# Decode attention beside a gated feed-forward on one core: the order of the first weights, narrower streams, and where a few transfers stand in the queue

## The chip, the core and the metric
The kernel runs on one of the eight cores of a Trainium2 chip. A core has a matrix engine (TensorE, in the profile PE, its weight loads PEld), a vector engine (VectorE, DVE), an engine for pointwise functions (ScalarE, ACT), a general engine (GpSimd, POOL) and one that mainly issues transfers (SyncE, SP). They run side by side and meet through semaphores. Sixteen DMA engines move data between the chip's memory and the core's SBUF; matmul results go to eight PSUM banks. The metric is device time in microseconds for one execution.

## The reference
Four decode requests (B = 4, one token each, D = 512). The token is normalised, and two branches start from it:

```python
xn = _layernorm(x, axis=-1)
# attention over the last W = 4096 positions, 32 query heads on 8 key/value heads
q = (xn @ wq)                                   # 512 -> 32*128
scores = einsum("bhqd,bhkd->bhqk", q, k) * (128 ** -0.5)
o = einsum("bhqk,bhkd->bhqd", softmax(scores), v)
A = o.reshape(4, 1, 4096) @ wo                  # 4096 -> 512
# gated feed-forward, F = 1792
Bf = (silu(xn @ w_gate) * (xn @ w_up)) @ w_down
out = x + A + Bf
```

All inputs and the output are bf16. What has to be read: 33.5 MB of keys, 33.5 MB of values, 4.2 MB each of `wq` and `wo`, 1.8 MB each of the three feed-forward matrices: 81 MB for very little arithmetic.

## The kernel before
The 32 pairs of request and key/value head are taken two at a time, in ND = 16 passes (two requests, one head). A pass d has a K tile and a V tile of 2 MB each: 64 blocks of 128 positions by 128 numbers. Both have two buffers in SBUF, bank d % 2.

**The preamble.** ScalarE and VectorE normalise x, TensorE transposes it into `XnT` (128 x 4 chunks, line 279). TensorE then forms gate (56 matmuls), up (56) and Q (128), each with a 128x128 block of weights as the stationary operand and `XnT` as the moving one. `XnT` is padded with zeros from the 4 columns that matter to WIDE = 64 columns, so each of these matmuls streams 64. Each writes 60 columns beyond its own into PSUM, zeros there, which accumulate without harm. VectorE then turns gate and up into the product `guT` (lines 280 to 288) and Q into the layout `QZ` (290 to 294); line 295 sets free the PSUM banks that gate and up have used, so that transposes may write there.

**The loop.** Eight rounds of two passes. On TensorE a pass is: wait for K of this pass; 32 transposes of the first half of K; the maxima of the pass before; PV of the second half of pass d - 2; the mask and 32 score matmuls; the shift of the pass before; 32 transposes of the second half; denominators and PV of the first half of pass d - 1; 32 score matmuls. VectorE copies each eight transposes out of PSUM (line 300), takes row maxima, and normalises. ScalarE does one exponential per pass. For the passes before the first one, P and V hold constants that GpSimd has written, and a signal from GpSimd (line 208) counts as their V having landed.

**SP's queue.** All big transfers are issued by SP, in the written order, and each wait holds up all that stands behind it (lines 225 to 248): W_gate, W_up, W_Q in two DMAs, K0, K1, the first half of V0, all without a wait; then a wait for the first PV of the loop (`s_pv` 1, since the second half's buffer is used up to then), the second half of V0; then in turn K of pass d, once the transposes of pass d - 2 are done (line 214, `s_tr`), and V of pass d - 1, once the PV of the pass two before it in its buffer is done (line 218, `s_pv`). Behind the loop come W_down, the last V in two halves, and W_O in four pieces of 16, 10, 4 and 2 rows of 128 KB (WO_CUTS, line 243).

**The tail.** TensorE adds x and the down-projection, finishes the last pass, transposes the attention output, and multiplies by W_O row by row as its pieces land (64 matmuls). VectorE rounds the sum, and two small transfers write the output.

## Time and profile before

| | |
|---|---|
| median of 3 runs | 200.82 us (200.08 to 201.39) |
| the profiled execution | 200.82 us, its span 198.3 us |
| granted TensorE clock, mean | 0.991 |
| HBM read | 81.01 MB, 409 GB/s over the span |
| TensorE busy | 170.0 us (86%) |
| VectorE busy | 112.1 us (57%) |
| ScalarE / GpSimd busy | 16.6 / 10.4 us |

The profile page is of one execution. It gives busy time by engine, the span in 40 slices (digits are tenths of a slice; below them the gigabytes per second moved), the chain of work that ended last, followed back from the end, the costliest groups of instructions with their count, busy time, mean duration and idle time ahead, and the issues of transfers with the time from issue to landing. Line numbers (L346 and so on) are those of the kernel; L346 is the helper `mm` through which nearly all matmuls go, so groups of that line are told apart by their tiles: `wq_sb`, `wg_sb`, `wu_sb` are the weights of Q, gate and up, `kbuf` and `vbuf` K and V, `kT` the transposed K, `ps_s` scores, `ps_o` PV. In a listing by time the columns are start, length, engine, line, operation, tiles, count, and in brackets the idle time ahead with its releaser. "SPq" is SP's queue: the time an issue takes there. A transfer lands when the last of its 16 parts has.

### The profile page before, as it was taken

How to read it: one execution, taken by the hardware profiler on the slowest of the kernel's cores; microseconds unless marked ns; L12 is line 12 of the kernel's file. 1: busy time of each engine (PE TensorE's matmuls, PEld its weight loads, DVE VectorE, ACT ScalarE, POOL GpSimd, SP SyncE). 2: the span in 40 equal slices, each digit the busy share in tenths (PEclk: the TensorE clock that was granted, in tenths of full speed). 3: DMA queues.
4: the chain of work that ended last, by engine and by line, in shares of the span. 5: the costliest groups of instructions: out<-in, count | busy, mean ns of one | idle time of the engine just before them, and what ended most of it. 6: DMA issues, size and time to landing. Idle time of an engine off the chain costs nothing.

```text
span 198.3 us, 8098 instructions
## 1 busy us (share of the span) xinstructions
PE 170.0 (86%) x3634; PEld 150.7 (76%) x3634; DVE 112.1 (57%) x246; ACT 16.6 (8%) x26; POOL 10.4 (5%) x23
## 2 busy tenths in 40 slices
PE   0383789999999989898989898989898989898865
PEld 0383778989889888887888788878887888786633
DVE  1010027777776867666667676767676767675110
ACT  6600001010101010100001010101010101010000
POOL 8920000000000000000000000000000000000000
PEclk9999999999999999999999999999999999999988
DMA  6999998999999999999999999999999999999991
GB/s 206 425 444 420 433 436 329 345 393 421 423 426 440 433 426 430 423 436 426 450 426 430 423 436 423 453 423 426 430 426 433 430 446 426 430 428 417 438 404 50
DMA packets 6223, 81.12 MB, mean 409 GB/s; under 512 B 700, under 2 KB 712, under 8 KB 968
## 3 DMA queue, kind: packets, MB, share of 16 engines
q1 hardware_dynamic: 6200, 81.01, 96.7%
q8 instruction: 6, 0.10, 0.2%
q10 hardware_dynamic: 16, 0.01, 0.0%
q14 instruction: 1, 0.01, 0.0%
HBM read 81.01 MB, written 0.00 MB: 409 GB/s over the span
## 4 chain that ended last, share of the span: by engine, by line
DMA 59%; PE 34%; issue 2%; SPq 2%; DVE 2%; DVEq 0%
DMA kbuf<-in_A_k_cache_dram 51%; PE ps_kt L384 17%; PE ps_s L346 9%; DMA wo_sb<-in_A_wo_dram 8%; PE ps_o L346 6%; PE ps_acc L346 2%; DVE kT L300 1%; SPq L229 1%; SPq L223 1%; SPq L245 0%; DVE y_sb L341 0%; SPq L225 0%; SPq L226 0%; DVEq L299 0%
## 5 line engine op out<-in xcount | busy, mean ns | idle before, releaser
L300 DVE COPY kT<-ps_kt 128x1024 bf16<-128x1024 bf16 x128 | 79.5, 684 | 21.4 <-PE ps_kt L384 21.3
L384 PE MATMUL ps_kt<-ident,kbuf 128*128 128x128 bf16 x1024 | 62.8, 220 | 8.0 <-DMA kbuf<-in_A_k_cache_dram 8.0
L384 PEld LDWEIGHTS ps_kt<-ident,kbuf 128*128 128x128 bf16 x1024 | 57.3, 98 | 13.1 <-issue 12.9
L346 PE MATMUL ps_o<-p,vbuf 128*128 128x64 bf16 x1120 | 38.6, 194 | 0.1
L346 PEld LDWEIGHTS ps_s<-qz,kT 128*128 128x128 bf16 x1024 | 31.4, 98 | 6.7 <-issue 3.6
L346 PEld LDWEIGHTS ps_o<-p,vbuf 128*128 128x128 bf16 x1120 | 35.3, 98 | 1.4 <-issue 0.2
L346 PE MATMUL ps_s<-qz,kT 128*128 x1024 | 34.7, 192 | 1.2
L265 ACT ACTIVATE p<-ps_s 128x512 bf16<-128x512 f32 x17 | 10.1, 597 | 161.2 <-PE ps_s L346 161.2
L305 DVE TENSOR_REDUCE rm<-ps_s 128x8 bf16<-128x512 f32 x17 | 11.8, 692 | 19.3 <-PE ps_s L346 19.3
L346 PE MATMUL ps_acc<-xnT,wq_sb 128*128 128x64 bf16 x128 | 7.2, 242 | 4.1 <-DMA wq_sb<-in_A_wq_dram 4.1
L346 PEld LDWEIGHTS ps_acc<-xnT,wq_sb 128*128 128x128 bf16 x128 | 6.9, 132 | 4.4 <-DMA wq_sb<-in_A_wq_dram 4.4
L346 PE MATMUL ps_o<-p,ones 128*128 128x128 bf16 (+1 forms) x69 | 6.9, 220 | 0.5 <-DVE qz L291 0.5
L316 DVE TENSOR_REDUCE den<-ps_o 128x8 f32<-128x128 f32 x18 | 4.9, 274 | 4.0 <-PE ps_o L346 4.0
L360 PE MATMUL ps_acc<-i,xn 4*128 4x4 f32 x4 | 0.6, 254 | 7.0 <-ACT xn L260 7.0
L291 DVE CAST qz<-ps_acc 128x64 bf16<-128x64 f32 x2 | 0.4, 220 | 11.0 <-PE ps_acc L346 11.0
L346 PE MATMUL ps_s<-dg,ones 8*128 8x512 bf16 x17 | 6.5, 385 | 0.0
L346 PE MATMUL ps_s<-mkc,mkr 2*128 2x512 bf16 x17 | 6.5, 385 | 0.0
L346 PE MATMUL ps_acc<-wo_sb,oP 128*4 128x256 bf16 x64 | 5.4, 339 | 1.3 <-DMA wo_sb<-in_A_wo_dram 1.3
L360 PEld LDWEIGHTS ps_acc<-i,xn 4*128 4x128 f32 x4 | 0.6, 208 | 7.0 <-issue 7.0
L346 PEld LDWEIGHTS ps_acc<-wo_sb,oP 128*4 128x4 bf16 x64 | 3.3, 102 | 3.3 <-DVE oP L339 1.4
L320 DVE TENSOR_TENSOR oT<-ps_o,den 128x8 f32 (+1 forms) x18 | 3.0, 167 | 4.2 <-issue 4.0
L346 PEld LDWEIGHTS ps_o<-p,ones 128*128 128x128 bf16 x69 | 4.6, 98 | 0.9 <-issue 0.9
(62 smaller groups left out, 60.1 us busy)
## 6 DMA issues: line engine op xcount, KB each, us to landing
kbuf<-in_A_k_cache_dram SPq DMA_DIRECT2D x16, 2048.0 KB, 12.6
vbuf<-in_A_v_cache_dram SPq DMA_DIRECT2D x14, 2048.0 KB, 11.2
wq_sb<-in_A_wq_dram SPq DMA_DIRECT2D x2, 2048.0 KB, 19.6
vbuf<-in_A_v_cache_dram SPq DMA_DIRECT2D x4, 1024.0 KB, 9.2
wo_sb<-in_A_wo_dram SPq DMA_DIRECT2D x1, 2048.0 KB, 14.3
wg_sb<-in_B_w_gate_dram SPq DMA_DIRECT2D x1, 1792.0 KB, 7.6
wu_sb<-in_B_w_up_dram SPq DMA_DIRECT2D x1, 1792.0 KB, 11.4
wd_sb<-in_B_w_down_dram SPq DMA_DIRECT2D x1, 1792.0 KB, 15.0
```

The lines of the kernel that those rows point to most:

```text
L223: eng.dma_start(VB[:, a:a + HKN], kv_ap(A_v_cache, d)[:, :, h * HKN:(h + 1) * HKN]).then_inc(done, 16)
L229: eng.dma_start(WQ[:, a:a + NC // 2 * HQ * Dh], wq_ap[:, a:a + NC // 2 * HQ * Dh]).then_inc(d_wq[h], 16)
L265: eng.activation(P[:, d % 2 * PS:d % 2 * PS + SN], ps_S[d % 2][:], ACT.Exp, scale=SCALE).then_inc(s_p, 1)
L291: last = eng.tensor_copy(QZ[:].rearrange("p (k b) c -> p k b c", b=2)[:, :, bp, 0:C].rearrange("p k (j h) -> p k j h", j=2), q_ps.rearrang ...
L300: eng.tensor_copy(KT[:, u * HKN + 1024 * g:u * HKN + 1024 * (g + 1)], kt_ps[g].rearrange("p a b -> p (a b)")).then_inc(s_ev, 1)
L305: eng.tensor_reduce(RM[:], ps_S[bank][:].rearrange("p (t c) -> p c t", c=C), AX.X, ALU.max).then_inc(s_rm, 1)
L316: eng.tensor_reduce(den[:], den_ps.rearrange("p (t c) -> p c t", c=C), AX.X, ALU.add)
L320: eng.tensor_tensor(OT[:, 2 * b:2 * b + 2, ds(r * REP, REP)], O_ps.rearrange("p (j h) -> p j h", j=2), den[:].rearrange("p (j h) -> p j h" ...
L346: return eng.matmul(o, l, r, start=start, stop=stop, skip_group_check=True)
L360: last = eng.transpose(xT_ps[:, c * B:(c + 1) * B], xn[:].rearrange("b (p c) -> b c p", c=NC)[:, c, :], I4[:])
L384: last = eng.transpose(kt_ps[g][:, k, :], KB[:, a:a + 128], ident[:])
```

## The change
Five things are changed together.

- W_Q is issued first and in one DMA, then W_gate and W_up. TensorE forms Q first, then gate and up, and VectorE lays out Q before it works on gate and up.
- `XnT` has 4 columns instead of 64, and the matmuls of Q, gate and up stream these 4. GpSimd no longer zeroes it.
- V of the second pass comes in two halves. The first half is issued when the scores of the first pass are done (`s_sc` 2), the other when V was issued before (`s_pv` 2). Each half has a semaphore, and GpSimd waits for both and then raises the semaphore for which TensorE waits.
- W_O is cut into five pieces (4, 12, 10, 4, 2 rows). The first, 4 rows, is issued behind the first half of V0, ahead of the wait for the loop's first PV.
- The remaining pieces follow at the end as before.

```diff
-    XnT = sb("xnT", [128, NC, WIDE], BF16)
+    XnT = sb("xnT", [128, NC, B], BF16)
...
-    WO_CUTS = (0, 16, 26, 30, 32)
+    WO_CUTS = (0, 4, 16, 26, 30, 32)
...
+    d_vy = [sem("d_vy%d" % h) for h in range(2)]
...
-            eng.memset(XnT[:].bitcast(FP32), 0.0)
...
             eng.engine_nop().then_inc(d_v[1], 32)
+            eng.wait_ge(d_vy[0], 16)
+            eng.wait_ge(d_vy[1], 16)
+            eng.engine_nop().then_inc(d_v[1], 16)
...
+            def load_wo(n):
+                a, b = WO_CUTS[n], WO_CUTS[n + 1]
+                eng.dma_start(WO[:, a:b, :], wo_ap[:, a:b, :]).then_inc(d_wo[n], 16)
+
+            eng.dma_start(WQ[:], wq_ap).then_inc(d_wq, 16)
             eng.dma_start(WG[:], wg_ap).then_inc(d_wg, 16)
             eng.dma_start(WU[:], wu_ap).then_inc(d_wu, 16)
-            for h in range(2):
-                a = h * NC // 2 * HQ * Dh
-                eng.dma_start(WQ[:, a:a + NC // 2 * HQ * Dh], wq_ap[:, a:a + NC // 2 * HQ * Dh]).then_inc(d_wq[h], 16)
             load_k(0)
             load_k(1)
 
             load_v_half(0, 0, d_v[0])
+            load_wo(0)
             eng.wait_ge(s_pv, 1)
             load_v_half(0, 1, d_v[0])
-            for d in range(2, ND):
+            load_k(2)
+            eng.wait_ge(s_sc, 2)
+            load_v_half(1, 0, d_vy[0])
+            eng.wait_ge(s_pv, 2)
+            load_v_half(1, 1, d_vy[1])
+            for d in range(3, ND):
                 load_k(d)
                 load_v(d - 1)
...
-            for n in range(len(d_wo)):
-                a, b = WO_CUTS[n], WO_CUTS[n + 1]
-                eng.dma_start(WO[:, a:b, :], wo_ap[:, a:b, :]).then_inc(d_wo[n], 16)
+            for n in range(1, len(d_wo)):
+                load_wo(n)
...
-            eng.tensor_copy(XnT[:, :, 0:B], xT_ps.rearrange("p (c b) -> p c b", b=B)).then_inc(s_xnT, 1)
-            eng.wait_ge(s_ex, 1)
-            (gate and up to guT: 7 lines)
+            eng.tensor_copy(XnT[:], xT_ps.rearrange("p (c b) -> p c b", b=B)).then_inc(s_xnT, 1)
             eng.wait_ge(s_q, 1)
             for bp in range(2):
                 last = eng.tensor_copy(
...
             last.then_inc(s_qz, 1)
+            eng.wait_ge(s_ex, 1)
+            (gate and up to guT: the same 7 lines)
             eng.engine_nop().then_inc(s_ev, NG)
...
-                        last = mm(o[:, t * B:t * B + WIDE],
+                        last = mm(o[:, t * B:(t + 1) * B],
                                   w[:].rearrange("p c (m t) -> p c t m", t=NF)[:, c, t, :], XnT[:, c, :],
...
+            eng.wait_ge(d_wq, 16)
+            for c in range(NC):
+                for h in range(HQ):
+                    a = (c * HQ + h) * Dh
+                    last = mm(q_ps[:, h * B:(h + 1) * B], WQ[:, a:a + Dh], XnT[:, c, :],
+                              start=(c == 0 and h == 0))
+            last.then_inc(s_q, 1)
             up_gate(WG, ps_kt[0], s_gate, d_wg)
             up_gate(WU, ps_kt[1], s_up, d_wu)
-            for c in range(NC):
-                if c % (NC // 2) == 0:
-                    eng.wait_ge(d_wq[c // (NC // 2)], 16)
-                for h in range(HQ):
-                    a = (c * HQ + h) * Dh
-                    last = mm(ps_acc[:, h * B:h * B + WIDE], WQ[:, a:a + Dh], XnT[:, c, :],
-                              start=(c == 0 and h == 0))
-            last.then_inc(s_q, 1)
```

More of the change, by code (lines that the diff above doesn't have):

```diff
@@ L113, in bass_parallel_sum__sliding_block_cached__swiglu_ffn__decode_kernel @@
     d_x = sem("d_x")
-    d_wq = [sem("d_wq%d" % h) for h in range(2)]
+    d_wq = sem("d_wq")
     d_wg = sem("d_wg")
@@ L278, in _ @@
             eng.wait_ge(s_const, 1)
-            eng.tensor_copy(XnT[:, :, 0:B], xT_ps.rearrange("p (c b) -> p c b", b=B)).then_inc(s_xnT, 1)
+            eng.tensor_copy(XnT[:], xT_ps.rearrange("p (c b) -> p c b", b=B)).then_inc(s_xnT, 1)
+            eng.wait_ge(s_q, 1)
+            for bp in range(2):
+                last = eng.tensor_copy(
+                    QZ[:].rearrange("p (k b) c -> p k b c", b=2)[:, :, bp, 0:C].rearrange("p k (j h) -> p k j h", j=2),
+                    q_ps.rearrange("p (k h b j) -> p k b j h", k=HKV, h=REP, b=2)[:, :, bp])
+            last.then_inc(s_qz, 1)
             eng.wait_ge(s_ex, 1)
@@ L288, in _ @@
             eng.tensor_tensor(guT[:], up_ps.rearrange("p (t b) -> p t b", b=B), gs[:], ALU.mult).then_inc(s_guT, 1)
-            eng.wait_ge(s_q, 1)
-            for bp in range(2):
-                last = eng.tensor_copy(
-                    QZ[:].rearrange("p (k b) c -> p k b c", b=2)[:, :, bp, 0:C].rearrange("p k (j h) -> p k j h", j=2),
-                    q_ps.rearrange("p (k h b j) -> p k b j h", k=HKV, h=REP, b=2)[:, :, bp])
-            last.then_inc(s_qz, 1)
             eng.engine_nop().then_inc(s_ev, NG)
```

## The prediction
> **What bounds the kernel now.** First the page's rows by slice, the traffic, and the chain that ended last.

> ```profile
> DMA  6999998999999999999999999999999999999991
> GB/s 206 425 444 420 433 436 329 345 393 421 423 426 440 433 426 430 423 436 426 450 426 430 423 436 423 453 423 426 430 426 433 430 446 426 430 428 417 438 404 50
> HBM read 81.01 MB, written 0.00 MB: 409 GB/s over the span
> DMA 59%; PE 34%; issue 2%; SPq 2%; DVE 2%; DVEq 0%
> ```

> The transfers are busy nearly from end to end, and 59% of the chain is theirs. Two slices of 4.96 us stand out, 329 and 345 GB/s (29.7 to 39.7 us); the rest holds about 430. Engine times by stretch, whose last three columns are the granted TensorE clock, the DMA share and GB/s, say it more sharply:

> ```profile
> 4.00:30.00 26.00, 16.67 (x266) 15.67 (x267) 3.11 (x11) 4.15 (x7) 7.21 (x6) 1.00 1.01 430
> 30.00:46.00 16.00, 15.82 (x357) 14.04 (x354) 12.00 (x27) 1.19 (x2) 0.00 (x0) 1.00 0.93 359
> 46.00:62.00 16.00, 15.92 (x358) 14.26 (x355) 11.44 (x26) 1.19 (x2) 0.00 (x0) 1.00 1.01 430
> 62.00:172.00 110.00, 101.24 (x2271) 90.77 (x2269) 75.11 (x158) 6.57 (x11) 0.00 (x0) 1.00 1.01 431
> ```

> From 62 to 172 us the traffic runs at 431 GB/s and TensorE is busy 101.2 of 110 us: transfers set the pace. From 30 to 46 us it is the other way round: TensorE has 15.82 of 16 us filled and traffic falls to 359. The shortfall is (431 - 359) x 16 us = 1.15 MB, or 2.7 us of transfer time. Why it idles is in SP's issues (start, length) and in the answers on the landing of single transfers (last column: us from issue to landing; x1 rows of a narrow window):

> ```profile
> 4.39 28.21 SPq L223 DMA_DIRECT2D vbuf<-in_A_v_cache_dram  x2
> 35.63 0.54 SPq L215 DMA_DIRECT2D kbuf<-in_A_k_cache_dram  x1
> 41.02 0.53 SPq L219 DMA_DIRECT2D vbuf<-in_A_v_cache_dram  x1
> ...
> kbuf<-in_A_k_cache_dram SPq DMA_DIRECT2D x1, 2048.0 KB, 25.7
> vbuf<-in_A_v_cache_dram SPq DMA_DIRECT2D x1, 1024.0 KB, 31.6
> vbuf<-in_A_v_cache_dram SPq DMA_DIRECT2D x1, 1024.0 KB, 7.2
> kbuf<-in_A_k_cache_dram SPq DMA_DIRECT2D x1, 2048.0 KB, 9.3
> ```

> The first half of V0 is issued at 4.39 and lands 31.6 us later, at 36.0; by then everything issued early is in. Its second half was issued at about 32.0 (7.2 us, landed 39.2), K2 only at 35.63 (landed 44.9), V1 at 41.02. From there nothing is lost any more: behind K2 come 81.01 MB less 16.25 MB (both gate and up matrices 3.67, W_Q 4.19, K0 to K2 6.29, V0 2.10) = 64.76 MB, and 64.76 / 0.431 = 150.3 us, so the last byte should land at 195.2. It does:

> ```profile
> 176.08 2.02 SPq L245 DMA_DIRECT2D wo_sb<-in_A_wo_dram  x4
> ...
> wo_sb<-in_A_wo_dram SPq DMA_DIRECT2D x1, 1280.0 KB, 16.7
> wo_sb<-in_A_wo_dram SPq DMA_DIRECT2D x1, 512.0 KB, 17.5
> wo_sb<-in_A_wo_dram SPq DMA_DIRECT2D x1, 256.0 KB, 17.7
> ...
> 193.49 2.52 PE ps_acc L346 x30
> ```

> The four issues take 0.5 us each, the last starts near 177.6 and lands 17.7 later, at 195.3. So **the end = landing of K2 + bytes behind it / 431 GB/s**, and the whole change comes down to those two terms. The last chain row shows the tail: rows 16 to 25 of W_O land at 193.45, 2.52 us of matmuls follow, then the output.

> The profiled execution took 200.82 us, of which 198.3 are the span and 2.5 lie around it; 200.82 is also the median of the three runs (200.08 to 201.39), so I subtract from it directly.

> **The change part by part.** *Four rows of W_O* (4 x 128 KB = 0.524 MB) move from behind K2 to ahead of the gated half of V0. At 431 GB/s that is 1.22 us less behind K2: 149.1 instead of 150.3. In front of K2 they land at 36.0 + 1.22 = 37.2, the gated half of V0 (1.049 MB, 2.43 us) no earlier than 39.7, K2 (2.097 MB, 4.87 us) no earlier than 44.5, if its issue stays at 35.63. If an issue into a drained queue sets it, the bounds are these: the first load of the kernel took 7.6 us for 1.835 MB,

> ```profile
> wg_sb<-in_B_w_gate_dram SPq DMA_DIRECT2D x1, 1792.0 KB, 7.6
> ```

> which is 7.6 - 4.26 = 3.3 us beside its bytes, and K2 itself 9.3 - 4.87 = 4.4. By 3.3 K2 can land at 43.8, by 4.4 at 44.9 as now. K2 thus stays between 44.5 and 44.9, and this part alone gives 1.2 to 1.6 us. Each extra issue costs SP 0.5 us at 5 us, where SP then waits till 32 anyway: nothing. Without that wait it would cost 0.5.

> The trace also bears on whether small pieces pay. The 512 KB piece of W_O, issued 0.5 us behind the 1280 KB piece, landed 0.5 + 17.5 - 16.7 = 1.3 us behind it; its bytes take 1.22. [...]

> *Second V in halves.* V1's first half is let go when the scores of the first pass are done, instead of with the second pass's PV. It waits for less than before, so nothing behind it on SP (its other half, then K3, whose own condition comes at 44.6) is held up. It puts 1.05 MB into the queue about 3 us earlier:

> ```profile
> 36.84 1.06 PE L346 MATMUL ps_s<-qz,kT 128*128 x32
> 53.40 0.39 PE L346 MATMUL ps_o<-p,ones 128*128 128x128 bf16 x4
> ```

> 37.9 instead of 41.0. V1 landed at 49.6 and is wanted by the third pass at 53.4, so it was never late, and its new detour over GpSimd's queue (two waits, one signal, nothing queued behind them) has 3.8 us of cover; bare it would cost a few tenths. It keeps the queue filled after K2, where the sum above finds no loss to win back: 0. With K2 late it is what keeps one loss from becoming two.

> *W_Q first, Q before gate and up.* The bytes ahead of K0 are the same 7.86 MB. What TensorE does last before the loop is now "up", not the second half of Q:

> ```profile
> 8.55 3.56 PE L346 MATMUL ps_kt<-xnT,wg_sb 128*128 128x64 bf16 x56 [0.90 <-DMA wg_sb<-in_B_w_gate_dram]
> 12.69 3.60 PE L346 MATMUL ps_kt<-xnT,wu_sb 128*128 128x64 bf16 x56 [0.58 <-DMA wu_sb<-in_B_w_up_dram]
> 19.27 3.59 PE L346 MATMUL ps_acc<-xnT,wq_sb 128*128 128x64 bf16 x64 [2.98 <-DMA wq_sb<-in_A_wq_dram]
> 23.95 3.60 PE L346 MATMUL ps_acc<-xnT,wq_sb 128*128 128x64 bf16 x64 [1.09 <-DMA wq_sb<-in_A_wq_dram]
> 28.88 1.96 PE L384 MATMUL ps_kt<-ident,kbuf 128*128 128x128 bf16 x32 [0.21 <-DMA kbuf<-in_A_k_cache_dram]
> 30.92 1.11 PE L346 MATMUL ps_o<-p,vbuf 128*128 128x64 bf16 x32
> ```

> The last weights landed at 23.95 and will again; "up" with 64 columns took 3.60, the same as half of Q. So the loop stays ready by 27.6 at worst, and its first transposes wait for K0 (3.09 + 25.7 = 28.8) either way. VectorE's gate arithmetic now sits ahead of the signal that frees the transposes' banks: one product of 0.2 us, done by 27.9. W_Q in one DMA saves an issue of 0.4 us that nobody waits for; one GpSimd memset less (0.2 us) likewise. All 0, hidden behind K0; without that cover they would be tenths.

> *Streaming 4 columns.* The matmuls before the loop can only get shorter (up to 3.6 us per group), and K0 hides that. But the rows above hold a trap. A matmul of one shape, 128x64, comes every 3.60 / 64 = 56 ns in Q and every 1.11 / 32 = 35 ns in the loop's PV, and one takes 242 against 194 ns:

> ```profile
> L346 PE MATMUL ps_acc<-xnT,wq_sb 128*128 128x64 bf16 x128 | 7.2, 242 | 4.1 <-DMA wq_sb<-in_A_wq_dram 4.1
> L346 PE MATMUL ps_o<-p,vbuf 128*128 128x64 bf16 x1120 | 38.6, 194 | 0.1
> ...
> 191.00:192.00 1.00, 1.00 (x18) 0.72 (x14) 0.00 (x0) 0.00 (x0) 0.00 (x0) 0.66 0.96 403
> 192.00:193.00 1.00, 1.00 (x12) 0.63 (x10) 0.00 (x0) 0.00 (x0) 0.00 (x0) 0.50 0.95 387
> 193.00:194.00 1.00, 0.94 (x11) 0.34 (x8) 0.00 (x0) 0.00 (x0) 0.00 (x0) 0.50 0.71 283
> 194.00:195.00 1.00, 1.00 (x16) 0.62 (x14) 0.00 (x0) 0.00 (x0) 0.00 (x0) 0.63 0.21 82
> 195.00:196.00 1.00, 0.99 (x20) 0.56 (x14) 0.00 (x0) 0.00 (x0) 0.00 (x0) 1.00 0.00 0
> ```

> The clock column reads 1.00 before the loop, but these durations say that TensorE runs slow there and is fast from the first transposes on. The tail shows what the slow state is: after little work (187 to 190.5) the granted clock is 0.50, and it comes back after (0.34 + 0.50 + 0.50 + 0.37) / 0.50 = 3.4 us of dense matmuls. Before the loop nothing but Q's second half, 3.6 us of unbroken 64-column streaming right ahead of it, is that dense. With 4 columns the array streams a sixteenth of this in each matmul, and I expect the loop to begin at half clock. One stretch of 3.4 us at half clock delays the first pass by 1.7 us; bounds: 0 (the array counts as busy all the same) and 3.4 (entry in mid-interval, two intervals lost). I take 1.7, the nearest row. [...]

> A first pass 1.7 us late moves the issue of K2 from 35.63 to 37.3, and K2 lands at 37.3 + 3.3 + 4.87 = 45.5 instead of 44.5: most of the cover is used up.

> **The sum.** K2 lands at 45.5, 0.6 later than now; 149.1 us of transfers follow instead of 150.3; the last byte lands at 194.6, the tail as now. 195.2 - 194.6 = 0.6 us: 200.82 - 0.6 = **200.2 us**, own range 199.3 to 201.1 (K2 at 44.6 to 46.4).

> **The rivals.**
> *Full clock at the loop's start:* K2 lands at 44.5 to 44.9, the gain is 1.2 to 1.6: 199.4 us. For it: weight loads run back to back and may count as work. Against: the bursts at 8.55 and 12.69, 3.6 us each and 0.6 us apart, did not raise the rate: Q at 19.27 still takes 56 ns a matmul.
> *A long slow start (the other side):* transposes of the first pass, half of its time, might not count as dense work, so that the clock comes back only after three intervals, 10.2 us. The pass is then 5.1 us late, K2 is issued at 40.7 and lands at 48.9; behind it 149.1: the end is 2.8 us later, 203.6 us. It decides from a delay of 2.3 us on (K2 at 46.1, where the 1.2 us of W_O are eaten up). Against it: in the tail one interval was enough, but that tail has no transposes.
> *A tail that does not follow, so that moving W_O does nothing:* 2.52 us of matmuls follow the landing of rows 16 to 25. Of these some 1.25 ran at half clock (193.49 to about 194.7), so their work is 1.9 us at full clock and 3.8 at half. Half throughout costs 1.3 us of the gain: with full clock at the start 200.7, with the forecast's start 201.5.
> *More than the sum:* the tail keeps its clock since rows 0 to 3 are in early and TensorE idles less before W_O; then only the last rows' matmuls, some 0.2 us, follow the last landing at 195.3, where now 0.7 do (193.49 + 2.52 = 196.0). With a full-clock start and K2 at 44.5 that is 1.6 + 0.5 = 2.1 us, 198.7 us.
> *Dear pieces:* the two added transfers each pay the 3.3 us that a first load pays beside its bytes: 206.8 us. Against it stands the 512 KB piece above, which paid 0.1.

> **How the numbers follow.** Chances: the forecast 0.44, full clock 0.23, slow start 0.14, the tail 0.10, more than the sum 0.08, dear pieces 0.01. A measurement of this kernel can tell about 1%, 2.0 us, from no change: the three runs alone span 1.3. Below 198.8 lie "more than the sum" and the lower edge of full clock with a better tail, 0.17; above 202.8 lie the slow start and the dear pieces, 0.15; within 1%, 0.68. The range 198.6 to 202.8 leaves about one in ten out at each end: it takes in K2's landing from 44.5 to 48 and the tail at either clock.

> **What would show it.** In the profile after: the 30 to 46 us stretch well above 359 GB/s (around 400 with the forecast, 430 with full clock); K2's landing near 45.5; the time between the first and the second 32 transposes of the first pass, which is now one row of 1.96 us and would be about 3.4 at half clock; the clock's first full stretch later than 29 us; V1's first half issued close behind the first pass's last scores; W_O's last landing 1.2 to 1.6 us plus K2's shift earlier than 195.3. I would be wrong if K0's landing were no longer what starts the loop, if the small transfers dented the rate (below 425 GB/s between 46 and 62), or if something other than K2's landing fixed the end, which the after-profile's last 150 us at 431 GB/s would deny or confirm.

## The result, and the profile after

The changed kernel takes 200.22 us, the median of 20 runs (199.01 to 201.68); the kernel before, in as many runs beside it, 201.57 us (200.08 to 203.62). The ratio is 0.9933 with a 95% interval of 0.9906 to 0.996: 0.7% faster, 1.35 us, less than the 1% that was called distinguishable beforehand, but the interval excludes no change. The time forecast was 200.2 us; the gain forecast was 0.6 us.

The two profiled executions alone would mislead: the one after took 200.81 us with a span of 199.0, the one before 200.82 us with 198.3. The profile before happened to be of a short span. In 72 further executions of the kernel before, run beside the experiments, the median span is 199.4 us (seven more, over 1.5% above the fastest, count as a slower state and are left out); the 20 of the changed kernel have 198.35. So in what follows one profile shows mechanisms, and only the timed runs show sizes.

From the page after, the rows that answer those shown of before: gigabytes per second in 40 slices, the traffic, the chain by engine.

```profile
GB/s 218 455 402 444 422 428 370 282 412 435 400 369 428 428 435 431 435 425 428 438 428 428 438 428 428 435 431 435 425 428 438 435 431 428 428 434 415 433 406 68
HBM read 81.01 MB, written 0.00 MB: 407 GB/s over the span
DMA 58%; PE 35%; issue 2%; SPq 2%; DVE 1%; DVEq 0%
```

The dip at 30 to 40 us is still there (370, 282), and there is a new, smaller one at 50 to 60 us (400, 369). The same stretches as before, with clock, DMA share and GB/s in the last three columns:

```profile
30.00:46.00 16.00, 15.92 (x314) 13.98 (x313) 10.67 (x24) 1.19 (x2) 0.00 (x0) 1.00 0.91 358
46.00:62.00 16.00, 15.55 (x368) 14.01 (x365) 11.70 (x26) 0.60 (x1) 0.00 (x0) 1.00 1.00 402
62.00:172.00 110.00, 101.69 (x2261) 91.09 (x2260) 75.53 (x159) 7.16 (x12) 0.00 (x0) 1.00 1.01 431
```

The first stretch moves as little as before, 358 against 359 GB/s, although four rows of W_O are in it; the second falls from 430 to 402. The listing by time shows why the first stretch gained nothing: Q, gate, up, the first and second 32 transposes of the loop, then the issues of V0's second half, K2 and V1.

```profile
13.26 3.56 PE L357 MATMUL ps_acc<-xnT,wq_sb 128*128 128x4 bf16 x128 [5.57 <-DMA wq_sb<-in_A_wq_dram]
17.40 3.52 PE L357 MATMUL ps_kt<-xnT,wg_sb 128*128 128x4 bf16 x56 [0.59 <-DMA wg_sb<-in_B_w_gate_dram]
22.94 3.52 PE L357 MATMUL ps_kt<-xnT,wu_sb 128*128 128x4 bf16 x56 [2.02 <-DMA wu_sb<-in_B_w_up_dram]
27.87 3.59 PE L394 MATMUL ps_kt<-ident,kbuf 128*128 128x128 bf16 x32 [0.64 <-DMA kbuf<-in_A_k_cache_dram]
35.18 1.96 PE L394 MATMUL ps_kt<-ident,kbuf 128*128 128x128 bf16 x32
...
33.51 0.54 SPq L226 DMA_DIRECT2D vbuf<-in_A_v_cache_dram  x1
37.17 0.54 SPq L218 DMA_DIRECT2D kbuf<-in_A_k_cache_dram  x1
39.47 3.63 SPq L226 DMA_DIRECT2D vbuf<-in_A_v_cache_dram  x2
```

The first 32 transposes take 3.59 us, those of the second half 1.96, and the first full clock that the trace records begins at 33.65 us, 5.8 us into the loop: it began at half clock. It started 1.0 us earlier than in the profile before (27.87 against 28.88, K0 being in sooner), and yet K2 is issued at 37.17, 1.5 us later. K2 landed 7.9 us after its issue, at 45.0:

```profile
kbuf<-in_A_k_cache_dram SPq DMA_DIRECT2D x1, 2048.0 KB, 7.9
```

The tail, first of the kernel before and then of the changed one (the last PV, the W_O matmuls, the rounding that ends TensorE's work):

```profile
185.06 2.03 PE L346 MATMUL ps_o<-p,vbuf 128*128 128x64 bf16 x64
190.56 5.44 PE L346 MATMUL ps_acc<-wo_sb,oP 128*4 128x256 bf16 x64 [1.27 <-DMA wo_sb<-in_A_wo_dram]
196.04 0.42 DVE L341 CAST y_sb<-ps_acc 128x256 bf16<-128x256 f32 x1 [6.27 <-PE ps_acc L346]
```
```profile
187.17 2.03 PE L357 MATMUL ps_o<-p,vbuf 128*128 128x64 bf16 x64
191.93 1.91 PE L357 MATMUL ps_acc<-wo_sb,oP 128*4 128x256 bf16 x32 [0.54 <-DVE oP L350]
194.41 2.31 PE L357 MATMUL ps_acc<-wo_sb,oP 128*4 128x256 bf16 x32 [0.57 <-DMA wo_sb<-in_A_wo_dram]
196.76 0.42 DVE L352 CAST y_sb<-ps_acc 128x256 bf16<-128x256 f32 x1 [4.88 <-PE ps_acc L357]
```

From the last PV to the rounding it was 10.98 us and is now 9.59: W_O's rows 0 to 15 no longer wait for a transfer but only for their other operand (the releaser is now "DVE oP"). That is where the gain is; in this one execution the last PV starts 2.1 us later than in the one before, and that eats it up.

### The profile page after: what moved, and what is told of

It reads as the page before. It is cut to its first block, busy times and chain, and to the rows that moved or that the text cites. A ratio compares the mean times of both kernels' runs of the same rounds, so it can differ in the third digit from the quotient of the medians.

```text
span 199.0 us, 8100 instructions
## 1 busy us (share of the span) xinstructions
PE 167.8 (84%) x3634; PEld 148.7 (75%) x3634; DVE 112.5 (57%) x246; ACT 16.6 (8%) x26; POOL 10.2 (5%) x22
## 3 DMA queue, kind: packets, MB, share of 16 engines
q1 hardware_dynamic: 6344, 81.01, 96.6%
HBM read 81.01 MB, written 0.00 MB: 407 GB/s over the span
## 4 chain that ended last, share of the span: by engine, by line
DMA 58%; PE 35%; issue 2%; SPq 2%; DVE 1%; DVEq 0%
DMA kbuf<-in_A_k_cache_dram 51%; PE ps_kt L394 18%; PE ps_s L357 9%; DMA wo_sb<-in_A_wo_dram 8%; PE ps_o L357 6%; PE ps_acc L357 2%; DVE kT L311 1%; SPq L226 1%; SPq L230 0%; SPq L234 0%; DVE y_sb L352 0%; SPq L232 0%; SPq L233 0%; DVEq L310 0%
## 5 line engine op out<-in xcount | busy, mean ns | idle before, releaser
L394 PE MATMUL ps_kt<-ident,kbuf 128*128 128x128 bf16 x1024 | 64.4, 222 | 8.7 <-DMA kbuf<-in_A_k_cache_dram 8.7
L394 PEld LDWEIGHTS ps_kt<-ident,kbuf 128*128 128x128 bf16 x1024 | 58.8, 99 | 14.1 <-issue 13.9
L357 PE MATMUL ps_o<-p,vbuf 128*128 128x64 bf16 x1120 | 39.3, 195 | 0.4 <-issue 0.4
L357 PEld LDWEIGHTS ps_o<-p,vbuf 128*128 128x128 bf16 x1120 | 36.0, 99 | 1.7 <-issue 0.5
L276 ACT ACTIVATE p<-ps_s 128x512 bf16<-128x512 f32 x17 | 10.1, 597 | 154.5 <-PE ps_s L357 154.5
L357 PE MATMUL ps_acc<-xnT,wq_sb 128*128 128x4 bf16 x128 | 3.6, 166 | 5.6 <-DMA wq_sb<-in_A_wq_dram 5.6
L357 PEld LDWEIGHTS ps_acc<-xnT,wq_sb 128*128 128x128 bf16 x128 | 3.5, 104 | 5.6 <-issue 5.6
L205 POOL MEMSET vbuf<- 128x6144 f32 x1 | 5.2, 5230 | 0.0
L357 PE MATMUL ps_kt<-xnT,wu_sb 128*128 128x4 bf16 x56 | 3.5, 199 | 2.0 <-DMA wu_sb<-in_B_w_up_dram 2.0
L357 PE MATMUL ps_acc<-wo_sb,oP 128*4 128x256 bf16 x64 | 4.2, 272 | 1.2 <-DMA wo_sb<-in_A_wo_dram 0.6
## 6 DMA issues: line engine op xcount, KB each, us to landing
kbuf<-in_A_k_cache_dram SPq DMA_DIRECT2D x16, 2048.0 KB, 12.6
vbuf<-in_A_v_cache_dram SPq DMA_DIRECT2D x13, 2048.0 KB, 11.3
vbuf<-in_A_v_cache_dram SPq DMA_DIRECT2D x6, 1024.0 KB, 9.0
wg_sb<-in_B_w_gate_dram SPq DMA_DIRECT2D x1, 1792.0 KB, 16.1
wu_sb<-in_B_w_up_dram SPq DMA_DIRECT2D x1, 1792.0 KB, 21.2
wd_sb<-in_B_w_down_dram SPq DMA_DIRECT2D x1, 1792.0 KB, 15.0
```

Of the source, the lines that this page charges most:

```text
L205: eng.memset(VB[:, HKN:].bitcast(FP32), 0.0)
L276: eng.activation(P[:, d % 2 * PS:d % 2 * PS + SN], ps_S[d % 2][:], ACT.Exp, scale=SCALE).then_inc(s_p, 1)
L357: return eng.matmul(o, l, r, start=start, stop=stop, skip_group_check=True)
L394: last = eng.transpose(kt_ps[g][:, k, :], KB[:, a:a + 128], ident[:])
```

## The experiments

The theory after the first profiles: **A**, thin streams leave TensorE at half clock when the loop begins, which makes the first pass late; the rows of W_O moved into the early gap pay for that and more. Against it: **B**, the half clock was an accident of one profile; **C**, the order and the narrow streams carry the gain, not the queue; **D**, the half clock costs nothing since transfers set the end. All ratios are to the kernel before, run on the same chip in the same session.

**The changed kernel again**, unedited.

> The changed kernel itself, on the same chip as the three beside it. Theory A (the first pass runs at half clock behind the 4-column stream, and the refilled queue pays for it): 0.990 to 0.996 of the kernel before, first 32 transposes in about 3.5 us, the clock's full stretch beginning after 31 us. Rival B (the half clock was an accident of one profile, and the gain is all from the queue): the first 32 transposes take 1.96 us here.

Measured: 0.992 (0.9888 to 0.9953). The first transposes were slow again, and K2 was issued 1.6 us behind where the wide variant below issues it:

```profile
27.78 3.44 PE L394 MATMUL ps_kt<-ident,kbuf 128*128 128x128 bf16 x32 [0.63 <-DMA kbuf<-in_A_k_cache_dram]
36.01 0.54 SPq L218 DMA_DIRECT2D kbuf<-in_A_k_cache_dram  x1
190.48 5.33 PE L357 MATMUL ps_acc<-wo_sb,oP 128*4 128x256 bf16 x64 [0.53 <-DVE oP L350]
```

B falls. The last row adds something: here the 64 W_O matmuls are one unbroken run of 5.33 us that starts as soon as its operand is there. The clock was at half for the middle 3.4 us of it (191.4 to 194.8), and TensorE, not the last landing, ended the kernel.

**The queue part alone.** On the kernel before:

```diff
-    WO_CUTS = (0, 16, 26, 30, 32)
+    WO_CUTS = (0, 4, 16, 26, 30, 32)
...
             load_v_half(0, 0, d_v[0])
+            load_wo(0)
             eng.wait_ge(s_pv, 1)
             load_v_half(0, 1, d_v[0])
+            load_k(2)
+            (V1 in halves, as in the change)
...
```

> The kernel before with the queue part alone: four rows of W_O behind the first half of V0, V1 in halves; Q, gate and up keep their order and 64 columns. Theory A: the first pass is at full clock whenever Q's last 3.6 us hold a whole clock interval, so this is as fast as the changed kernel or faster, 0.985 to 0.994. Rival C (order and narrow streams carry the gain): 0.997 to 1.003.

Measured: 0.9939 (0.9913 to 0.9964). With old order and 64 columns nearly the whole gain is there: C falls. The first transposes take 1.96 us and K2 goes out at 34.28, though its landing at 45.8 was late.

**The changed kernel without the queue part** (the same lines taken back, order and 4 columns kept).

> The changed kernel without the queue part: W_Q first, 4 columns, but V1 whole and W_O all at the end. Theory A: every execution begins the loop at half clock and has no cover, so it is slower than the changed kernel by 1.2 to 2.5 us, and level with the kernel before or slower, 0.998 to 1.008. Rival C: 0.990 to 0.996, as the changed kernel.

Measured: 0.9997 (0.9975 to 1.0019). Order and narrow streams together show no gain; against the changed kernel it lacks 0.7%, 1.4 us, as A has it.

**Narrow streams alone.** On the kernel before:

```diff
-    XnT = sb("xnT", [128, NC, WIDE], BF16)
+    XnT = sb("xnT", [128, NC, B], BF16)
...
-                        last = mm(o[:, t * B:t * B + WIDE],
+                        last = mm(o[:, t * B:(t + 1) * B],
...
-                    last = mm(ps_acc[:, h * B:h * B + WIDE], WQ[:, a:a + Dh], XnT[:, c, :],
+                    last = mm(ps_acc[:, h * B:(h + 1) * B], WQ[:, a:a + Dh], XnT[:, c, :],
```

> The kernel before with 4 columns in Q, gate and up and nothing else changed. Theory A (thin streams leave the clock at half when the loop begins, always, while 64 columns leave it so in a part of the executions): first 32 transposes 3.4 to 3.6 us, time 1.000 to 1.010 of the kernel before. Rival (columns do not matter): 0.997 to 1.003 with first transposes of 1.96 us.

Measured: 1.0008 (0.9975 to 1.0041). The mechanism is there (first transposes 3.59 us, K2 issued at 36.86), a loss beyond 0.4% is excluded, and none is shown.

**The wide variant: the changed kernel with 64 columns.** Run twice, in two sessions.

```diff
-    XnT = sb("xnT", [128, NC, B], BF16)
+    XnT = sb("xnT", [128, NC, WIDE], BF16)
...
+            eng.memset(XnT[:].bitcast(FP32), 0.0)
...
-                        last = mm(o[:, t * B:(t + 1) * B],
+                        last = mm(o[:, t * B:t * B + WIDE],
...
-                    last = mm(q_ps[:, h * B:(h + 1) * B], WQ[:, a:a + Dh], XnT[:, c, :],
+                    last = mm(ps_acc[:, h * B:h * B + WIDE], WQ[:, a:a + Dh], XnT[:, c, :],
```

> The changed kernel with 64 columns again in Q, gate and up. Q is then 6.8 us of unbroken dense streaming from about 13 us, gate and up follow almost without a break, so by theory A the clock is full before the loop in every execution and the first 32 transposes take 1.96 us; K2 is issued about 1.5 us earlier than the 37.2 us of the changed kernel, and the time is 0.984 to 0.991 of the kernel before. Rival D (the half clock costs nothing, since the transfers set the end): the same as the changed kernel within 0.2%.

> The wide variant once more (64 columns in Q, gate and up, all else as in the changed kernel), for a tighter interval and a second look at the clock with another phase: 0.985 to 0.990, first 32 transposes 1.96 us, K2 issued near 34.4 us.

Measured: 0.9881 (0.9847 to 0.9916) and 0.9915 (0.9884 to 0.9946). Both times the loop began at full clock. Of the first run, in the listing by time the first transposes, the issue of K2 and the W_O matmuls; then K2's landing (10.5 us after the issue), the stretch from 30 to 46 us, and three stretches ahead of the loop:

```profile
27.65 1.96 PE L395 MATMUL ps_kt<-ident,kbuf 128*128 128x128 bf16 x32 [0.80 <-DMA kbuf<-in_A_k_cache_dram]
34.39 0.54 SPq L219 DMA_DIRECT2D kbuf<-in_A_k_cache_dram  x1
...
189.51 5.33 PE L358 MATMUL ps_acc<-wo_sb,oP 128*4 128x256 bf16 x64 [0.53 <-DVE oP L351]
```
```profile
kbuf<-in_A_k_cache_dram SPq DMA_DIRECT2D x1, 2048.0 KB, 10.5
```
```profile
30.00:46.00 16.00, 15.30 (x358) 13.61 (x355) 10.92 (x25) 1.19 (x2) 0.00 (x0) 1.00 1.00 410
...
22.00:24.00 2.00, 1.27 (x21) 1.28 (x22) 0.91 (x3) 0.12 (x1) 0.00 (x0) 0.75 0.99 426
24.00:26.00 2.00, 2.00 (x37) 2.00 (x36) 0.00 (x0) 0.00 (x0) 0.00 (x0) 0.50 1.02 434
26.00:28.00 2.00, 1.20 (x15) 0.66 (x13) 0.91 (x2) 0.00 (x0) 0.00 (x0) 0.90 0.98 418
```

K2 goes out 1.6 to 2.8 us before the changed kernel's two profiles, and the gap from 30 to 46 us is smaller (410 GB/s, and 391 in the second run's profile, against 358 and 392). The full clock was not held all the way: in the first run it fell to half at 23.0 us, behind a wait of 0.86 us between gate and up, and was back at 26.4, 1.25 us ahead of the loop. In the second run, without that wait, it stayed full up to the tail: the mean of 0.991 over 197.8 us leaves room for 3.6 us at half, and the tail has 3.4 of them. The variant beats the kernel before in both sessions. Against the changed kernel it is ahead where both ran in one session (0.9881 beside 0.992); in the other session it has 0.9915, where the changed kernel's 20 runs elsewhere gave 0.9933. That is some 0.3% on average, and the intervals overlap: that it beats the changed kernel is likely and not shown, so D is not settled. And K2 lands at 44.9, where the changed kernel has 45.0 and 44.3: a K2 issued earlier did not land earlier.

**Which stream holds the clock.** The wide variant with 4 columns in gate and up, 64 in Q:

```diff
-                                  ...[:, c, t, :], XnT[:, c, :],
+                                  ...[:, c, t, :], XnT[:, c, 0:B],
```

> The changed kernel with 64 columns in Q and 4 in gate and up. Q's dense streaming from 13 us brings the clock to full by about 20 us; then follow 3.5 us of gate, a wait of about 2 us, 3.5 us of up, all thin. If a thin stream counts as idle, the clock is back at half before 28 us, the first 32 transposes take 3.4 to 3.6 us and the time is that of the changed kernel, 0.990 to 0.995. If weight loads back to back count as work, the clock holds, the transposes take 1.96 us and the time is that of the wide variant, 0.985 to 0.990.

Measured: 0.9922 (0.9895 to 0.995). Stretches of 2 us (after the comma the busy time of PE and PEld; the last three columns are clock, DMA share, GB/s):

```profile
18.00:20.00 2.00, 2.00 (x53) 2.00 (x51) 0.30 (x2) 0.00 (x0) 0.00 (x0) 1.00 1.00 430
20.00:22.00 2.00, 2.00 (x36) 2.00 (x36) 0.05 (x1) 0.00 (x0) 0.00 (x0) 1.00 1.01 421
22.00:24.00 2.00, 2.00 (x36) 2.00 (x36) 0.65 (x2) 0.22 (x1) 0.00 (x0) 0.55 1.03 442
24.00:26.00 2.00, 2.00 (x36) 2.00 (x36) 0.27 (x2) 0.00 (x0) 0.00 (x0) 0.50 1.05 451
```

and in the listing by time the first transposes:

```profile
27.79 3.59 PE L395 MATMUL ps_kt<-ident,kbuf 128*128 128x128 bf16 x32 [0.63 <-DMA kbuf<-in_A_k_cache_dram]
```

**The two halves of the queue part**, each on the changed kernel: V1 whole again, and all of W_O at the end.

```diff
-            load_k(2)
-            (V1 in halves)
-            for d in range(3, ND):
+            for d in range(2, ND):
```
```diff
-    WO_CUTS = (0, 4, 16, 26, 30, 32)
+    WO_CUTS = (0, 16, 26, 30, 32)
...
-            load_wo(0)
...
```

> The changed kernel with four rows of W_O ahead but V1 whole again. Theory (the rows of W_O carry the queue's gain, 1.22 us, and V1's halves matter only when the first pass is late, which it is here): between the changed kernel (0.992) and the one without the queue part (1.000), 0.993 to 0.997.

> The changed kernel with V1 in halves but all of W_O at the end. By the prediction the halves win back nothing by themselves when K2 is on time, and up to 1 us where the first pass is 1.7 us late: 0.995 to 1.000. Together with the run of W_O alone: the two parts add up to the 0.8% between the kernel without the queue part and the changed one.

Measured: with W_O's rows alone 0.9928 (0.9898 to 0.9957), with V1's halves alone 0.9978 (0.9955 to 1.0001). The rows of W_O carry the gain; the halves at most 0.45%, and nothing that shows on top of the rows.

**V1 whole in the wide variant** (the first of the two diffs above, on the wide variant).

> The wide variant with V1 in one transfer: four rows of W_O ahead, order and all else kept. By the prediction the halves of V1 are worth nothing when the first pass is on time: level with the wide variant, 0.985 to 0.991. If they carry part of the gain, 0.991 to 0.995.

Measured: 0.9915 (0.9883 to 0.9948), the same number as the wide variant beside it. At full clock the halves are worth nothing that can be measured.

**Eight rows ahead instead of four**, on the changed kernel:

```diff
-    WO_CUTS = (0, 4, 16, 26, 30, 32)
+    WO_CUTS = (0, 8, 16, 26, 30, 32)
```

> The changed kernel, 4 columns, with eight rows of W_O ahead instead of four: 0.52 MB more, 1.22 us of transfers, in front of K2. With the first pass at half clock the queue of the changed kernel runs dry for about 1.4 us ahead of K2; if that idle time is what the half clock costs, eight rows fill it and the time falls by 0.5 to 1.2 us against the changed kernel, 0.986 to 0.990. If the later lack (a queue that runs dry again behind V1, at 54 us) or the tail on TensorE sets the end, it is the same as the changed kernel, 0.990 to 0.995.

Measured: 0.9933 (0.9894 to 0.9972); no gain over four rows in the median. The profile shows where a further gain would go:

```profile
187.05 2.03 PE L357 MATMUL ps_o<-p,vbuf 128*128 128x64 bf16 x64
191.81 5.26 PE L357 MATMUL ps_acc<-wo_sb,oP 128*4 128x256 bf16 x64 [0.53 <-DVE oP L350]
```

The W_O matmuls run without a wait for any transfer. From the last PV there is a chain on TensorE and VectorE of 10.1 us to the rounding, and transfers that are finished sooner than this no longer help; the last landing was at 195.0, TensorE ended at 197.1. The granted clock was at half for 3.4 us of it, from 191.7; at full clock the W_O matmuls would take some 3.8 us instead of 5.26 (an estimate, twice the 1.91 us of 32 in the changed kernel's profile), and the chain some 8.6. The timed executions fall into two groups by this: six list a mean granted clock of 1.000 and have a median of 199.1 us, six list 0.991 and have 201.0. In the changed kernel's 28 the two medians are 199.8 (20) and 200.7 (8). So eight rows may well pay where the tail keeps its clock; eight rows together with a tail that is made to keep it were not run.

**Keeping the clock in the tail.** The wide variant with eight spare matmuls between the last PV and W_O, streaming into a bank that is no longer read:

```diff
             pv(1, 1, None)
+            def fill(k):
+                for _ in range(k):
+                    mm(ps_S[0][:], ones[:], KB[:, 0:512], start=True)
+            fill(3)
             eng.wait_ge(s_nrm, ND + 2)
...
             last.then_inc(s_t4, 1)
+            fill(1)
...
             last.then_inc(s_pm, 1)
+            fill(4)
```

> The changed kernel with 64 columns in Q, gate and up, and eight spare 512-column matmuls in the three waits between the last PV and W_O, into a bank that nobody reads any more. Theory (the tail of the wide variant is set by TensorE, whose clock falls to half at 190 to 194 us): the clock stays full, the 64 W_O matmuls no longer take 5.33 us but end with the last landing near 193.9, and the time falls by 0.5 to 1.0 us against the wide variant, 0.983 to 0.987 of the kernel before. Rival (the last landing sets the end): level with the wide variant, 0.986 to 0.990.

Measured: 0.9892 (0.9851 to 0.9933), level with the wide variant. The filling does what it should, the granted clock being 1.00 from 187 to 197 us, and the end stays where it was:

```profile
190.36 1.91 PE L358 MATMUL ps_acc<-wo_sb,oP 128*4 128x256 bf16 x32
192.47 2.31 PE L358 MATMUL ps_acc<-wo_sb,oP 128*4 128x256 bf16 x32 [0.20 <-DMA wo_sb<-in_A_wo_dram]
```

32 matmuls in 1.91 us, full clock; then the other rows are waited for, and the last landing, 194.4 in this execution, ends the kernel. With four rows ahead the two limits of the tail, transfers and TensorE, lie about half a microsecond apart (in the first profile of the wide variant the last landing was at 193.9 and TensorE ended at 194.8; had it waited for the landing as here, it would have ended some 0.5 us sooner), so that lifting one alone gives little.

The profiles side by side (one execution each; us; "tail" is from the start of the last 64 PV matmuls to the rounding):

| kernel | ratio | first 32 transposes | K2 issued | last PV starts | tail |
|---|---|---|---|---|---|
| before | 1 | 1.96 | 35.6 | 185.1 | 11.0 |
| changed | 0.9933 | 3.59 | 37.2 | 187.2 | 9.6 |
| changed, again | 0.992 | 3.44 | 36.0 | 185.7 | 10.1 |
| queue part alone | 0.9939 | 1.96 | 34.3 | 185.6 | 10.1 |
| without the queue part | 0.9997 | 3.59 | 36.6 | 185.9 | 11.5 |
| narrow alone | 1.0008 | 3.59 | 36.9 | 186.1 | 12.2 |
| wide variant | 0.9881 | 1.96 | 34.4 | 184.8 | 10.1 |
| wide variant, again | 0.9915 | 1.96 | 34.6 | 185.5 | 10.1 |
| W_O's rows alone | 0.9928 | 3.59 | 37.0 | 186.5 | 9.6 |
| V1's halves alone | 0.9978 | 3.59 | 36.7 | 186.4 | 11.1 |

Where four rows are ahead, the tail is 9.6 to 10.1 us; where they are not, 11.0 to 12.2. The start of the last PV scatters by 2.4 us over these ten executions, and by 1.5 us between the two of the changed kernel alone, so that no row of the table gives the size of an edit by itself.

## Why the prediction was right, and where it was off

*The 1.2 to 1.6 us of W_O's rows:* right in place and size. With the rows (0.9928) against without (0.9997), all else equal, it is 0.7% or 1.4 us (each against the kernel before of its own session); with V1 in halves on both sides (0.9933 and 0.992 against 0.9978) it is 0.9 to 1.2 us. Some of it may come by a way the sum did not have. The prediction took "the tail as now"; but with rows 0 to 15 in before their operand, TensorE idles less ahead of W_O (0.53 to 0.54 us in the nine profiles with rows ahead and no filling, 1.27 to 1.82 in the four without rows), and the clock more often stays full there. Of the 28 timed executions of the changed kernel 20 list a mean granted clock of 1.000 (with narrow streams that mean begins near 31 to 34 us, so what lowers it is the tail); of the 36 of the three variants with narrow streams and no rows ahead (narrow alone, without the queue part, V1's halves alone) 7 do. The rival "more than the sum" had this. The rival of a tail that does not follow had its other half: in four profiles with rows ahead (the second of the changed kernel, the queue part alone, the first of the wide variant, eight rows) the W_O matmuls ran through half clock without a wait, and TensorE, not a transfer, ended the kernel.

*Half clock at the start of the loop:* right, and every profile with thin gate and up shows it: the first 32 transposes take 3.44 to 3.59 us in these eight, and 1.96 in the six with 64 columns. The delay was taken as 1.7 us, with bounds of 0 and 3.4. From the first transposes of the loop to the issue of K2 it is 6.75 us in the six profiles that begin at full clock, and 8.2 to 9.3 in the eight that begin at half: a delay of 1.5 to 2.6 us, since full clock came 3.1 to 5.8 us into the loop and not always after the 3.4 that the tail of the profile before had shown. The half clock lasted 3.4 us in each of the eight tails where a profile shows it whole (before, the changed kernel again, the queue part alone, without the queue part, V1's halves alone, the wide variant twice, eight rows), at least 6.6 us in the tail of narrow alone (from 190.4 to past 197.0), and 10.2 us ahead of and in the loop with a wide Q (from 22.2 to 32.4). That it goes by intervals, and that it matters where one begins, as the upper bound, the long slow start and what was expected of the queue part alone have it, was the author's estimate from the tail before; no run shows where an interval begins. The rival of a long slow start, 10.2 us at half clock in the loop and a delay of 5.1 us, did not come, though its threshold of 2.3 us was reached in three profiles. That K2 was issued at 37.17 in the first profile, as forecast (37.3), is luck: the loop began 1.0 us earlier and its first pass was 2.55 us late, where the sum had 0 and 1.7.

What failed is the next step, **"the end = landing of K2 + bytes behind it / 431 GB/s"** with K2 landing at issue + 3.3 + 4.87. K2's landing hardly follows its issue: issued at 34.39 it took 10.5 us, at 36.01 8.3 us, at 37.17 7.9 us, and landed at 44.9, 44.3 and 45.0. With an early issue the last of its 16 parts is late for a reason that is not known: its first part is in at 42.1 in the wide variant and at 44.4 in the changed kernel, and the last one at 44.9 and 45.0. And the end does not follow K2's landing: 45.0 + 149.1 gives 194.1, and the last byte landed at 196.3.

Counted in bytes the end comes out. Up to 46 us this execution moved at the same mean rate as the one before (382 GB/s in both), the four rows of W_O included, so nothing was won there; from 46 to 62 us it lacks 28 GB/s (402 against 430), 0.45 MB or 1.0 us; from 62 to 172 us both have 431. And 195.3 + 1.0 = 196.3. The prediction had named both among the signs of being wrong, a rate below 425 GB/s from 46 to 62 us and an end that something other than K2's landing fixes, and both came (402 and 414 GB/s in the changed kernel's two profiles). What makes this second gap is open: the three profiles with V1 whole and no rows ahead have 428 to 432 there, the others 400 to 433, and it is not the late pass alone, since the second profile of the wide variant, on time, has 411. The prediction had looked for losses behind K2 in the profile before, found none, and carried that over.

*The size of the gain:* forecast 0.6 us, measured 1.35 us (0.8 to 1.9 by the interval of the ratio, which leaves the forecast out). The terms by measurement: 0.9 to 1.4 us from W_O's rows, where the sum had 1.6; the half clock costs 0.2 us by the run of narrow streams alone (its interval reaches from a gain of 0.5 to a loss of 0.8), 0.1 us by the run with a wide Q beside the second wide one, and 0.4 to 0.8 us by the wide variant against the changed kernel, where the sum had 1.0. So the mis-sized term is the price of the half clock. One reservation: in the profile before, the first full clock that the trace records begins at 27.48 us, 1.4 us ahead of the loop; whether other executions of the kernel before begin the loop at half clock too is not on record, and if some do, the run of narrow streams alone shows too small a price. That the forecast time of 200.2 us came out is in part luck: it was counted off from 200.82, and more runs put the kernel before at 201.57. The chances do not quite fit their range either: with 0.17 below 198.8 and 0.15 above 202.8 the range leaves out more than one in ten at each end.

*Order, one W_Q transfer, 4-column matmuls of Q:* forecast 0 behind the landing of K0; 0.9997 for all of this together with the narrow gate and up, without the queue part, agrees, but it is a sum. The order was never run alone. The wide variant and the queue part alone differ only in the order and the single W_Q transfer, and have 0.9881 and 0.9915 against 0.9939: the order may be worth 0.2 to 0.6% (the intervals overlap), and the half clock may take back as much. No profile shows where such a gain would lie (both issue K2 at 34.3 to 34.6), so this rival stays open. The reason given, K0 at 28.8 either way, did not hold: K0 is in by 27.4 to 27.9 in every other profile, with old order and new.

*V1's halves:* forecast 0, at most a help when the pass is late. 0.9978 with the halves alone and no difference on top of the rows agree.

*Dear pieces:* nothing of it is seen. A price of 3.3 us for each added transfer would have made the queue part a loss, and it is the gain: four rows in a piece of 512 KB, queued behind another transfer, gave 0.9 to 1.4 us.

**What stays open.** Why the last part of a K2 that is issued early lands so late. Transfers of instructions, 16 KB and 0.88 to 0.97 us each, six in the span, share the DMA engines (page, queue q8); that one of them makes the part of its engine late is the author's estimate from these times, and was not tried. These runs do not resolve what the half clock costs in time, somewhere from 0 to 0.8 us, nor whether the order is worth anything, nor what lowers the traffic from 46 to 62 us.

## What to carry to other kernels

A few hundred kilobytes that are needed at the end can cost little if they are loaded into a gap that exists anyway (four rows of W_O, 0.52 MB, gave 0.9 to 1.4 us here), and what they save is read at the tail, as long as the last compute chain is not the longer one (eight rows gave no more than four in the median, where a tail at half clock ended the kernel). Padding gate and up to 64 columns cost nothing that shows (3.5 to 3.6 us for 56 matmuls with either width), and all six profiles here in which the matmuls right ahead of the loop were padded began the loop at full clock, with 32 transposes in 1.96 us; that this saves time was not shown. And before a forecast is counted off from one profile, compare that execution's span with others: here it was 1.1 us below their median, nearly as large as the effect.

## What the runs showed of the hardware that had not been expected

A matmul with 4 columns instead of 64 came twice as fast in Q (3.56 us for 128, 28 ns each, against 56) and no faster in gate and up (3.52 us for 56, 63 ns each, against 64). The factor of two in Q belongs to the half clock: in the run of the queue part alone the first half of Q, with 64 columns, took 2.04 us for 64 matmuls, 32 ns each; and the loop's 128x64 PV matmuls, 32 at a time, took 1.89 us, 59 ns each, just ahead of the change to full clock at 33.65 us in the first profile of the changed kernel, and 1.11 us, 35 ns each, at full clock. Gate and up took 3.5 to 3.6 us in every profile, at either clock (with a wide Q, gate 3.50 us and mostly at 1.00, up 3.52 us and at 0.50). Q's weights lie next to each other; those of gate and up are every 14th column, and their weight loads take about 160 ns against 104:

```profile
L357 PEld LDWEIGHTS ps_acc<-xnT,wq_sb 128*128 128x128 bf16 x128 | 3.5, 104 | 5.6 <-issue 5.6
```
```profile
L358 PEld LDWEIGHTS ps_kt<-xnT,wg_sb 128*128 128x128 bf16 x56 | 3.4, 160 | 0.0
```

(The first row is of the changed kernel, the second of the variant with a wide Q.) That the step of 14 is the cause is argued from this; no run changed the layout. The column of the granted clock reads 1.00 until the first change of clock that the profile records, whatever the clock was before it: in the first profile of the changed kernel it reads 1.00 from 28 to 32 us, where 32 transposes take 3.59 us, against 1.96 for the next 32. Durations of a known shape tell the truth there.
